# An attention and two-layer kernel: the first token pair in three blocks of 256 tokens, split out of PSUM, with four value buffers

## The chip, the cores and the metric

The kernel runs on one core of a Trainium2 chip. The core has TensorE (PE: matmuls and transposes into PSUM), VectorE (DVE), ScalarE (ACT), GpSimd (POOL) and SyncE (SP), which mostly issues DMAs; 16 DMA engines move data between device memory and the on-chip SBUF. Each engine works through its own list of instructions in order. The metric is the device time of one execution in microseconds (us); less is better.

## What is computed

Local attention with memory tokens, then two gated feed-forward layers, all in float32:

```python
# q, k, v: 4 x 8 heads x 768 x 64; mem_k, mem_v: 4 x 8 x 8 x 64
for c in range(768 // 32):                      # chunks of 32 queries
    k_full = [mem_k, k[32c-16 : 32c+40]]        # 8 + 56 keys, cut at the ends
    a = softmax(q_c @ k_full.T / 8); out_c = a @ v_full
x = out as 3072 tokens x 512
h = x @ w_in                                    # 512 -> 2048
x = (h * tanh(softplus(h))) @ w_out             # 2048 -> 512
xn = rms_norm(x) * rms_g
y = (silu(xn @ w_gate) * (xn @ w_val)) @ w_out2 # 512 -> 1536 -> 512
```

## The kernel before

**Precision.** A float32 operand is split into a high part rounded to fp32r and a low part that is the rest (`split`: ACT casts, DVE subtracts). A product of two operands is three matmuls: high x high, high x low, low x high (`product`, lines 639 to 641).

**Stages.** The 3072 tokens are four pairs of 768. For each pair attention runs in six tiles of 128 tokens and is followed by `x @ w_in`, whose result goes to device memory (`g_scratch`). The first pair uses plain products; pairs 2 to 4 use a scheme with seven products in place of eight on sums of blocks (`group1`), for which the operands are summed and split beforehand (`t_pieces`, the products 1, 6, 5, 4, 2, 7, 3 in this order). The later layers follow and don't concern the change. While PE works on one pair, the attention of the next is strung between its products (`slots`).

**Attention of tile t, step by step.** The names are used in all that follows.
- k, q, v loads (`load_k`, `load_q`, `load_v`; SP): 256-byte rows; a v tile is eight DMAs and, for some tiles, two of mem_v (8 KB each), which POOL then copies to three more places (`mem_v_copy`, line 385). k and q have two buffers each, v has two (`vw`).
- K (`k_pe`, line 395) and Q (line 438): four transposes each on PE into a bank; ACT and DVE copy them out (lines 404 to 412, 449). K of tile t + 1 completes the keys of tile t.
- S (line 458): scores, 64 small matmuls. DVE takes the maximum and subtracts (471, 472), ACT takes exp (477).
- P (line 490): four transposes; ACT copies (497).
- V (line 506): weights times values. DVE normalises (519 to 522).
- E (line 532): four transposes back. ACT copies them into the block `xb` (539).
K, Q, P and E share two PSUM banks (bk_86 and bk_87 in the order's rows, called `bk` in the trace), S and V share bkp.

**Products of the first pair.** A block is 384 tokens, three tiles. After its last E, `x_split` splits it in two halves of 256 features (four instructions of 768 columns). `unit(b, i)` multiplies block b by 256 columns of `w_in` (i = 0 to 7): 24 matmuls of 384 columns into two banks and two evictions by ACT (line 691). Three units of block 0 are strung into the attention of the first pair (`NHEAD`, `HEADS`), the other 13 run with the attention of pair 2 between them.

**Weights.** `w_in` is read as raw 64-bit halves of 512 KB (`load_raw`, issued by POOL, two buffers). The conversion `cv_all` takes each raw tile through ACT (202, 205), DVE (209, 210, 216) and a split (153, 154). Raw tiles are numbered here as they are loaded: 0 and 1 belong to i = 0, 2 and 3 to i = 1, and so on. In the first pair's attention six are converted (`CV_START` = 24 steps, four each).

**What sets the order.** A scheduler orders the instructions of each engine from the order in which the program emits them, by a timeline of its own; an instruction in `pin` keeps its place among pinned ones.

## Time and profile before

| | |
|---|---|
| time, median of 3 runs (least to most) | 1167.13 us (1166.1 to 1167.37) |
| the profiled execution: its time, its span | 1167.72 us, 1166.0 us |
| PE busy | 1140.7 us, 98% of the span |
| DVE, ACT, POOL busy | 823.8, 629.2, 183.4 us |
| mean granted clock of TensorE | 0.993 |

A busy PE is not always PE at its peak: the granted clock and the spacing of its instructions have to be read as well. The profile's rows give the start of an instruction or of a run of equal ones, how long they were on, and in square brackets how long the engine had been idle ahead of it and what released it. Starts are counted from the first instruction of the span.

### The profile page before, as it was taken

How to read it: one execution, taken by the hardware profiler on the slowest of the kernel's cores; microseconds unless marked ns; L12 is line 12 of the kernel's file. 1: busy time of each engine (PE TensorE's matmuls, PEld its weight loads, DVE VectorE, ACT ScalarE, POOL GpSimd, SP SyncE). 2: the span in 40 equal slices, each digit the busy share in tenths (PEclk: the TensorE clock that was granted, in tenths of full speed). 3: DMA queues.
4: the chain of work that ended last, by engine and by line, in shares of the span. 5: the costliest groups of instructions: out<-in, count | busy, mean ns of one | idle time of the engine just before them, and what ended most of it. 6: DMA issues, size and time to landing. Idle time of an engine off the chain costs nothing.

```text
span 1166.0 us, 22910 instructions
## 1 busy us (share of the span) xinstructions
PE 1140.7 (98%) x9052; PEld 1005.2 (86%) x9052; DVE 823.8 (71%) x1254; ACT 629.2 (54%) x1008; POOL 183.4 (16%) x165
## 2 busy tenths in 40 slices
...
GB/s 195 187 219 224 191 300 260 240 297 284 170 302 290 255 225 144 188 354 157 195 375 409 123 349 316 355 407 359 312 363 356 329 283 319 180 160 145 145 91 37
DMA packets 213276, 294.20 MB, mean 252 GB/s; under 512 B 104240, under 2 KB 160560, under 8 KB 204336
## 3 DMA queue, kind: packets, MB, share of 16 engines
...
## 4 chain that ended last, share of the span: by engine, by line
PE 75%; DMA 9%; DVE 8%; ACT 5%; issue 2%; POOL 0%; SPq 0%; ACTq 0%; DVEq 0%; POOLq 0%
PE bk L639 13%; PE bk L640 13%; PE bk L641 13%; DMA s<-g_scratch 4%; PE bk L912 4%; PE bk L914 4%; PE bk L913 4%; PE bk L755 3%; PE bk L756 3%; PE bk L754 3%; DVE T L154 2%; PE bkp L639 2%; PE bkp L640 2%; PE bkp L641 2%; PE bkp L506 2%
## 5 line engine op out<-in xcount | busy, mean ns | idle before, releaser
L639 PE MATMUL bk<-T,w 128*128 128x384 f32 (+1 forms) x860 | 315.6, 369 | 1.3 <-ACT c L657 1.0
L640 PE MATMUL bk<-T,w 128*128 128x384 f32 (+1 forms) x860 | 311.2, 362 | 0.0
L641 PE MATMUL bk<-T,w 128*128 128x384 f32 (+1 forms) x860 | 307.4, 361 | 0.0
L639 PEld LDWEIGHTS bk<-T,w 128*128 128x128 f32 x860 | 162.0, 189 | 21.0 <-ACT c L657 1.3
L640 PEld LDWEIGHTS bk<-T,w 128*128 128x128 f32 x860 | 161.9, 188 | 16.5 <-DVE T L154 0.3
L641 PEld LDWEIGHTS bk<-T,w 128*128 128x128 f32 x860 | 161.5, 188 | 15.8
L912 PE MATMUL bk<-w,T 128*128 128x256 f32 x396 | 112.1, 283 | 0.2 <-ACT T L153 0.2
L913 PE MATMUL bk<-w,T 128*128 128x256 f32 x396 | 112.0, 283 | 0.0
L914 PE MATMUL bk<-w,T 128*128 128x256 f32 x396 | 111.9, 283 | 0.0
L755 PE MATMUL bk<-T,w 128*128 128x512 f32 x276 | 107.5, 390 | 0.5 <-DVE T L154 0.5
L756 PE MATMUL bk<-T,w 128*128 128x512 f32 x276 | 107.1, 389 | 0.0
L754 PE MATMUL bk<-T,w 128*128 128x512 f32 x276 | 105.8, 389 | 0.0
L669 POOL TENSOR_TENSOR v<-c,v 128x512 f32<-128x512 f32 x36 | 54.1, 1503 | 291.7 <-DVE c L665 259.0
L665 DVE TENSOR_TENSOR c<-bk,c 128x512 f32<-128x512 f32 (+2 forms) x72 | 43.0, 598 | 54.5 <-PE bk L641 41.9
L912 PEld LDWEIGHTS bk<-w,T 128*128 128x128 f32 x396 | 76.0, 192 | 0.5 <-ACT T L153 0.4
L913 PEld LDWEIGHTS bk<-w,T 128*128 128x128 f32 x396 | 76.0, 192 | 0.0
L914 PEld LDWEIGHTS bk<-w,T 128*128 128x128 f32 x396 | 75.9, 192 | 0.0
L649 ACT COPY c<-bk 128x512 f32<-128x512 f32 (+2 forms) x72 | 36.9, 514 | 69.1 <-PE bk L641 25.3
L154 DVE TENSOR_TENSOR T<-s,T 128x1024 fp32r<-128x1024 f32 (+1 forms) x50 | 62.5, 1258 | 15.2 <-ACT T L153 15.1
L782 ACT ACTIVATE s<-s 128x1024 f32<-128x1024 f32 x44 | 46.4, 1059 | 31.3 <-DMA s<-g_scratch 31.2
L755 PEld LDWEIGHTS bk<-T,w 128*128 128x128 f32 x276 | 51.8, 188 | 11.6 <-DVE T L154 0.9
L756 PEld LDWEIGHTS bk<-T,w 128*128 128x128 f32 x276 | 51.8, 188 | 10.8
...
## 6 DMA issues: line engine op xcount, KB each, us to landing
...
```

Of the source, the lines that this page charges most:

```text
L154: keep((eng or nc.vector).tensor_tensor(lo, src, hi.bitcast(F32), op=ALU.subtract))
L639: nc.tensor.matmul(ps, whi, xh, start=first and kk == 0, stop=False, **more)
L640: nc.tensor.matmul(ps, whi, xl, start=False, stop=False, **more)
L641: nc.tensor.matmul(ps, wlo, xh, start=False, stop=kk == 1, **more)
L669: nc.gpsimd.tensor_tensor(c22, u3, z5, op=ALU.add)
L754: nc.tensor.matmul(ps, ahi, bhi, start=start, stop=False)
L755: nc.tensor.matmul(ps, ahi, blo, start=False, stop=False)
L756: nc.tensor.matmul(ps, alo, bhi, start=False, stop=stop)
L782: nc.scalar.activation(x, g, self.act)
L912: nc.tensor.matmul(ps, t[:, 0, f], w[:, 0], start=first and f == 0, stop=False, **more)
L913: nc.tensor.matmul(ps, t[:, 0, f], w[:, 1], start=False, stop=False, **more)
L914: nc.tensor.matmul(ps, t[:, 1, f], w[:, 0], start=False, stop=f == HG - 1, **more)
```

## The change

- The first pair becomes three blocks of 256 tokens (`NS`), two tiles each. A unit has 24 matmuls of 256 columns, into one bank, and one eviction of 512 columns (`unit_parts`); there are 24 units.
- The result of E is split straight out of PSUM by tile and half (`x_part`: one cast, one subtraction of 256 columns each); `xb` and `x_split` are not used in this pair.
- Two more value buffers, `v2`, lie in weight slot 1, which is free until its weights are converted; v2 and v3 go there. These two tiles load and copy mem_v as tiles 0 and 1 do.
- The start is emitted step by step from the list `START`. Each word is a step and its arguments: `lk lq va vb lr` are loads of k, q, the halves of v and raw weights; `K Q S P V E` are the steps above; `ka kb km kd qc pc` are copies out of PSUM; `mx sb ex z`, `nr nm` are parts of S's and V's follow-up; `mv` copies mem_v; `a` to `e` are the five steps of a conversion (ACT's two, DVE's two, DVE's add, ACT's cast, DVE's subtraction); `hi lo` are the split; `U.b.i` is a quarter of a unit, `g` its eviction, `st` its store. None of it is pinned.
- Eight raw tiles are converted in the start (`N_EARLY`), and six units run there: (0,0), (0,1), (1,1), (1,0), (1,2), (0,2). The other 18 follow with pair 2's attention, in an order of their own.

The bodies of `att_b1`, `att_d1` and `k_ev` are cut into parts with names and otherwise unchanged; this is left out of the diff.

```diff
-    jobs, raws, n_load, n_raw, start = [], [], [0], [10 ** 6], [True]
+    jobs, raws, n_load, n_raw, start = [], [], [0], [10 ** 6], [False]
...
+    def plain_steps(key, u, n):
+        raw = raws.pop(0)
+        if n == 0:
+            wslot[key] = w_slot(u)
+        w = as7(wslot[key])
+        hi, lo = (w[:, n:n + 3:2, l, :].rearrange("p e (k f) -> p k e f", k=2) for l in range(2))
...
+                if kind == "plain":
+                    done += 1
+                    if done <= N_EARLY:
+                        continue
+                    cv_prefetch(done - 1)
+                    steps = plain_steps(key, u, n)
+                    for c in "abcde":
+                        steps[c]()
+                        if c == "b":
+                            cv_prefetch(done)
+                        yield
+                    continue
                 cv_prefetch(done)
...
+    VS = NP * 4 * (D + 1)
+    v2 = w_slot(1)[:, 0:2 * VS].bitcast(F32)
+    v2 = [v2[:, VS * u:VS * u + VS].rearrange("p (a c d) -> p a c d", a=NP, c=4) for u in range(2)]
...
-    def load_v(t):
+    def load_v(t, halves=(0, 1)):
         b, i = divmod(t, SPB)
         s0 = 128 * i
-        vt = vw[t % 2]
-        vn[t] = vt
-        for h2 in range(2):
+        vt = vn[t] = v2[t - 2] if t in (2, 3) else vw[t % 2]
+        for h2 in halves:
             p0 = 64 * h2
-            if i < 2:
+            if i < 2 or t in (2, 3):
...
+    def att_c2(t):
+        att_c1(t)
+        mem_v_copy(t)
+
+    def att_d2(t):
+        att_d(t)
+        if t + 2 < TSUB:
+            load_v(t + 2)
...
-    def x_split(b, half):
-        t = t_new()
-        split(xb[b][:, 2 * half:2 * half + 2, :], t[:, 0], t[:, 1])
-        xtab[b, half] = t
-
-    xtab, n_unit = {}, [0]
+    NS = 256
+    NBS = 2 * N // NS
+    xs0 = []
+
+    def x_piece(b, half, l):
+        if not xs0:
+            xs0.extend(t_new().rearrange("p l a n -> p (l a n)") for _ in range(4))
+        t, at = (xs0[2 * b + half], 2 * NS * l) if b < 2 else (xs0[2 * half + l], 4 * NS)
+        return t[:, at:at + 2 * NS].rearrange("p (k n) -> p k n", k=2)
+
+    def x_part(t, half, l):
+        b, r = divmod(t, NS // 128)
+        src = st_e[t][:, 2 * half:2 * half + 2, :]
+        hi = x_piece(b, half, 0)[:, :, 128 * r:128 * r + 128]
+        if l == 0:
+            nc.scalar.copy(hi, src)
+        else:
+            lo = x_piece(b, half, 1)[:, :, 128 * r:128 * r + 128]
+            nc.vector.tensor_tensor(lo, src, hi.bitcast(F32), op=ALU.subtract)
+
+    n_unit, g_unit = [0], {}
...
+    def unit_parts(b, i):
+        w = wtab["i", i]
+        ps = bk[n_unit[0] % 4]
+        n_unit[0] += 1
+
+        def mul(e, half):
+            x = [x_piece(b, half, l) for l in range(2)]
+            ws = w[:, 2 * e + half].rearrange("p l (k f) -> p l k f", k=2)
+            out_ = ps[:, NS * e:NS * e + NS]
+            for kk in range(2):
+                end = half and kk
+                nc.tensor.matmul(out_, ws[:, 0, kk, :], x[0][:, kk, :],
+                                 start=not (half or kk), stop=False)
+                nc.tensor.matmul(out_, ws[:, 0, kk, :], x[1][:, kk, :], start=False, stop=False)
+                nc.tensor.matmul(out_, ws[:, 1, kk, :], x[0][:, kk, :], start=False, stop=bool(end))
+
+        def evict():
+            g = gp.tile([128, 2, N], F32, tag="g", name="g")[:, :, 0:NS]
+            nc.scalar.copy(g, ps.rearrange("p (e n) -> p e n", e=2))
+            g_unit[b, i] = g
+
+        dst = g_d[2 * i:2 * i + 2, :, NS * b:NS * b + NS].rearrange("f p n -> p f n")
+        return [lambda e=e, half=half: mul(e, half) for e in range(2) for half in range(2)], evict, dst
...
+    for n, x in enumerate(vw + v2):
+        if n < 2:
+            nc.gpsimd.memset(x, 0.0)
         nc.gpsimd.memset(x[:, :, :, D:D + 1], 1.0)
...
+    N_EARLY = 8
...
+    START = """
+        lk.0 lk.1 lq.0 lq.1 va.0 K.0 lr.0 ka.0 km.0 K.1 lr.1 kb.0 lk.2 kd.1 ka.1 km.1 Q.0 vb.0
+        kb.1 qc.0 Q.1 S.0 lk.3 va.1 qc.1 mx.0 a.0 sb.0 ex.0 b.0 lq.2 K.2 lq.3 z.0 vb.1 c.0 P.0
+        ka.2 mv.0 kd.2 S.1 d.0 kb.2 e.0 pc.0 K.3 lk.4 a.1 mx.1 va.2 kd.3 sb.1 Q.2 ka.3 b.1 V.0
+        ex.1 qc.2 vb.2 c.1 kb.3 mv.1 nr.0 P.1 d.1 nm.0 Q.3 pc.1 e.1 S.2 lr.2 lq.4 E.0 va.3 qc.3
+        mx.2 hi.0.0 K.4 sb.2 hi.0.1 mv.2 lo.0.0 ka.4 V.1 lo.0.1 ex.2 kd.4 vb.3 kb.4 nr.1 P.2
+        lr.3 a.2 nm.1 Q.4 S.3 pc.2 b.2 lk.5 E.1 qc.4 va.4 mx.3 hi.1.0 c.2 hi.1.1 mv.3 lo.1.0 d.2
+        lo.1.1 U.0.0 vb.4 a.3 sb.3 U.0.0 e.2 lr.4 ex.3 V.2 b.3 va.5 P.3 nr.2 K.5 lr.5 pc.3 c.3
+        U.0.0 ka.5 nm.2 U.0.0 d.3 lk.6 kd.5 V.3 kb.5 e.3 lq.5 g.0.0 vb.5 E.2 a.4 nr.3 U.0.1 nm.3
+        U.0.1 hi.2.0 b.4 hi.2.1 E.3 st.0.0 S.4 lk.7 hi.3.0 lo.2.0 lr.6 hi.3.1 lo.2.1 U.0.1
+        lo.3.0 lq.6 Q.5 lo.3.1 rg mx.4 U.0.1 lq.7 qc.5 c.4 K.6 g.0.1 U.1.1 sb.4 lk.8 d.4 st.0.1
+        U.1.0 kd.6 ex.4 e.4 S.5 a.5 P.4 mx.5 U.1.1 pc.4 b.5 U.1.0 U.1.1 sb.5 lr.7 U.1.0 c.5 ex.5
+        V.4 d.5 z.5 P.5 a.6 va.6 nr.4 U.1.1 e.5 U.1.0 nm.4 pc.5 U.1.2 b.6 g.1.1 V.5 g.1.0 vb.6
+        c.6 E.4 U.0.2 nr.5 hi.4.0 hi.4.1 nm.5 U.1.2 d.6 lo.4.0 U.0.2 st.1.1 a.7 lo.4.1 st.1.0
+        E.5 e.6 va.7 U.0.2 hi.5.0 b.7 U.1.2 hi.5.1 U.0.2 lo.5.0 lo.5.1 U.1.2 vb.7 g.0.2 c.7
+        g.1.2 d.7 e.7 st.0.2 st.1.2
+    """
...
+    with ExitStack():
+        for word in START.split():
+            name, *args = word.split(".")
+            start_ops[name](*map(int, args))
+    start[0] = True
+    cv_n[0] = 5 * N_EARLY
...
-    CV_I = 64
+    CV_I = 80
...
-    units = [(1, i) for i in range(NHEAD)]
-    units += [(b, i) for i in (3, 4, 7, 5, 6) for b in range(2)]
+    units = [(2, 0), (2, 2), (2, 3), (2, 1), (1, 3), (0, 3), (0, 4), (1, 4), (2, 4), (0, 7), (1, 7), (2, 7), (0, 5), (1, 5), (2, 5), (2, 6), (0, 6), (1, 6)]
     at = {u: 4 * n + 4 for n, u in enumerate(units)}
     more = {}
-    finish_at(more, 7, at[1, 7] + 1)
-    bt = slots((att_list(1), 4 * len(units)), (0, 73), tail_of(1), calls(more), CV_I)
+    finish_at(more, 7, max(at[b, 7] for b in range(NBS)) + 1)
+    bt = slots((att_list(1), 4 * len(units)), (0, 91), tail_of(1), calls(more), CV_I)
```

The order that the change gives, at three places. In the first, on POOL at the start of the program, `raw` is a raw weight tile and `COPY` a copy of mem_v. Before:

```order
L149 DMA raw<-in_moe_w_in_dram 128x2x512 x2
L931 MEMSET vw 128x16 x2
L385 COPY vw<-vw 8x4x195 x3
L149 DMA raw<-in_moe_w_in_dram 128x2x512
L385 COPY vw<-vw 8x4x195
L149 DMA raw<-in_moe_w_in_dram 128x2x512 x4
```

After (`w` is the weight slot that holds v2 and v3):

```order
L423 COPY vw<-vw 8x4x195
L149 DMA raw<-in_moe_w_in_dram 128x2x512
L423 COPY vw<-vw 8x4x195
L149 DMA raw<-in_moe_w_in_dram 128x2x512
L423 COPY vw<-vw 8x4x195 x2
L149 DMA raw<-in_moe_w_in_dram 128x2x512
L423 COPY w<-w 8x4x195 x3
L149 DMA raw<-in_moe_w_in_dram 128x2x512
L423 COPY w<-w 8x4x195
L149 DMA raw<-in_moe_w_in_dram 128x2x512 x4
```

Raws 2, 3, 4, 5 and 6 now each stand behind a copy of mem_v; before, raw 2 stands behind three, raw 3 behind one, and raws 4 to 6 behind none.

The second place is ACT late in the start, where the first unit's eviction comes (`g<-bk0_82`). Before, with `ca` and `lr` the two first steps of a conversion, `xb` the copy behind E, `p` an exp, `pT` the copy behind P:

```order
L202 ACTIVATE ca_735<-raw_549 128x512
L205 ACTIVATE lr_737<-raw_549 128x512
L691 COPY g_740<-bk0_82 128x384
L539 COPY xb_800<-bk4_86 128x4x128
L691 COPY g_740<-bk1_83 128x384
L477 ACTIVATE p_780<-p_780 128x512
L691 COPY g_875<-bk2_84 128x384
L153 CAST w_736<-ca_735 128x2x2x128
```

After, with raw_774 raw 6, raw_899 raw 7, and `CAST T` the high parts behind an E step:

```order
L200 ACTIVATE ca_948<-raw_774 128x512
L203 ACTIVATE lr_949<-raw_774 128x512
L452 COPY kw_108<-bk5_87 128x4x32
L793 COPY g_695<-bk0_82 128x2x256
L200 ACTIVATE ca_1059<-raw_899 128x512
L219 CAST w_947<-ca_948 128x2x2x128
L203 ACTIVATE lr_1060<-raw_899 128x512
L768 CAST T_426<-bk4_86 128x2x128
L768 CAST T_427<-bk4_86 128x2x128
L219 CAST w_947<-ca_1059 128x2x2x128
L793 COPY g_810<-bk1_83 128x2x256
```

Two raw tiles' conversions now stand among the first eviction, the casts that free bank 86 (bk4_86) and the second eviction; bank 86 is the one into which PE's next step, Q of tile 5, transposes.

The third place is PE where the first pair ends and `group1` begins (lines 639 to 641 before, 717 to 719 after, for its products). Before; the last E of pair 2 stands 24 products ahead of the first row of `kn`:

```order
L641 MATMUL bk3_85<-T_963,w_1914 128x384
L395 MATMUL bk5_87<-ident_89,kn_1758 128x128
L438 MATMUL bk4_86<-ident_89,qn_1571 128x128 x4
L395 MATMUL bk5_87<-ident_89,kn_1758 128x128 x3
L639 MATMUL bk0_82<-T_2129,w_1491 128x384
L640 MATMUL bk0_82<-T_2129,w_1491 128x384
L641 MATMUL bk0_82<-T_2129,w_1491 128x384
L639 MATMUL bk0_82<-T_2129,w_1491 128x384
L640 MATMUL bk0_82<-T_2129,w_1491 128x384
L641 MATMUL bk0_82<-T_2129,w_1491 128x384
L639 MATMUL bk1_83<-T_2145,w_1491 128x384
L640 MATMUL bk1_83<-T_2145,w_1491 128x384
```

After; the last E of pair 2 stands 20 products ahead of the first row with 384 columns:

```order
L789 MATMUL bk3_85<-T_427,w_1961 128x256
L717 MATMUL bk0_82<-T_2349,w_1442 128x384
L718 MATMUL bk0_82<-T_2349,w_1442 128x384
L719 MATMUL bk0_82<-T_2349,w_1442 128x384
L717 MATMUL bk0_82<-T_2349,w_1442 128x384
L718 MATMUL bk0_82<-T_2349,w_1442 128x384
L719 MATMUL bk0_82<-T_2349,w_1442 128x384
L433 MATMUL bk5_87<-ident_89,kn_1743 128x128 x4
L492 MATMUL bk4_86<-ident_89,qn_1747 128x128 x4
L717 MATMUL bk1_83<-T_2364,w_1442 128x384
L717 MATMUL bk2_84<-T_2373,w_1442 128x384
L718 MATMUL bk1_83<-T_2364,w_1442 128x384
```

K and Q move behind the first group product; T_2145 and T_2364 are the operands of the second one (product 6), whose low part is read by the matmul of line 640 before, 718 after.

## Rows read from the trace of the kernel before

**Rows 1.** The page, busy time, share of the span and instructions of each engine.
```profile
PE 1140.7 (98%) x9052; PEld 1005.2 (86%) x9052; DVE 823.8 (71%) x1254; ACT 629.2 (54%) x1008; POOL 183.4 (16%) x165
```

**Rows 2.** Stretches: length, busy us (x instructions) by engine, PE clock, DMA share, GB/s.
```profile
0.00:20.00 20.00, 11.73 (x224) 8.45 (x224) 4.18 (x10) 7.86 (x15) 5.89 (x15) 0.83 0.85 188
...
20.00:40.00 20.00, 13.41 (x376) 9.81 (x360) 13.65 (x27) 13.13 (x26) 4.34 (x5) 0.83 1.01 199
...
40.00:60.00 20.00, 18.60 (x354) 16.59 (x339) 13.22 (x27) 11.30 (x21) 1.45 (x2) 0.91 0.93 198
...
80.00:100.00 20.00, 20.00 (x317) 18.68 (x323) 11.54 (x24) 13.06 (x26) 2.89 (x4) 1.00 0.88 205
```

**Rows 3.** PE in order: start us, us, line, output<-inputs, count [idle before <-released by].
```profile
4.17 1.09 PE L395 MATMUL bk<-ident,kn 128*128 128x128 f32 x4 [4.17 <-DMA kn<-in_mem_k_dram]
...
31.27 0.63 PE L395 MATMUL bk<-ident,kn 128*128 128x128 f32 x4 [1.65 <-DMA kn<-in_k_dram]
...
42.85 0.87 PE L506 MATMUL bkp<-vw,pT 64*32 64x65 f32 x50 [0.79 <-DMA vw<-in_v_dram]
...
44.42 1.63 PE L639 MATMUL bk<-T,w 128*128 128x384 f32 x4
...
49.64 0.86 PE L458 MATMUL bkp<-kw,qT 64*32 64x64 f32 x64
...
50.43 0.66 PE L532 MATMUL bk<-ident,x 128*128 128x128 f32 x4
...
50.85 0.42 PE L640 MATMUL bk<-T,w 128*128 128x384 f32 x1
```

**Rows 4.** PE in order, at 75 us (384 columns) and 1050 us (256 columns).
```profile
75.05 0.33 PE L639 MATMUL bk<-T,w 128*128 128x384 f32 x1
...
76.09 0.33 PE L639 MATMUL bk<-T,w 128*128 128x384 f32 x1
...
1050.39 0.28 PE L912 MATMUL bk<-w,T 128*128 128x256 f32 x1
...
1051.11 0.28 PE L912 MATMUL bk<-w,T 128*128 128x256 f32 x1
```

**Rows 5.** DMA queues, first 65 us (packets, MB, share); raw weight tiles to landing.
```profile
q1 hardware_dynamic: 31474, 8.28, 69.1%
...
q0 software_dynamic: 1104, 4.06, 20.8%
...
DMA to landing us min/median/max: 4.4/5.4/7.3
```

**Rows 6.** POOL, ACT and DVE in order of time, same columns as rows 3.
```profile
11.88 0.82 POOL L385 COPY vw<-vw 8x780 f32<-8x780 f32 x1 [7.07 <-DMA vw<-in_mem_v_dram]
...
37.49 0.62 ACT L153 CAST w<-ca 128x512 fp32r<-128x512 f32 x1 [1.02 <-DVE ca L216]
...
39.43 0.67 ACT L205 ACTIVATE lr<-raw 128x512 int32<-128x512 uint32 x1
...
35.48 0.43 DVE L209 TENSOR_SCALAR ca<-ca 128x512 int32<-128x512 int32 x1 [1.31 <-ACT ca L202]
...
35.94 0.69 DVE L210 SCALAR_TENSOR_TENSOR ca<-raw,ca 128x512 int32<-128x512 int32 x1
...
154.44 0.40 ACT L153 CAST w<-sm 128x256 fp32r<-128x256 f32 x1
...
153.09 0.41 DVE L300 TENSOR_TENSOR sm<-ca,sm 128x256 f32<-128x256 f32 x1
```

**Rows 7.** PE and DVE in order of time where the token pair ends.
```profile
137.35 0.60 PE L532 MATMUL bk<-ident,x 128*128 128x128 f32 x4
...
141.78 0.34 PE L641 MATMUL bk<-T,w 128*128 128x384 f32 x1
...
144.22 0.44 PE L640 MATMUL bk<-T,w 128*128 128x384 f32 x1
...
143.22 0.94 DVE L154 TENSOR_TENSOR T<-g,T 128x768 fp32r<-128x768 f32 x1
```

223 lines of the change are left out of this document (127 added, 96 removed).

## The prediction, made before the changed kernel ran

> **What bounds the kernel now.** I read the page first, then the stretches, then PE's instructions in order of time. PE is busy for 98% of the span [rows 1]. By stretches it is not full only at the start: 11.7 and 13.4 us busy of 20 in the first two, at a granted clock of 0.83, and all of 20 from 80 us on [rows 2]. Behind the start PE has no gap worth the name, so a microsecond that PE loses or saves before about 140 us is lost or saved at the end. The reader should see in PE's rows what the start waits for: PE's first instruction comes at 4.17 us, k5 is awaited until 31.27, v3 until 42.85, and the first block product runs at 44.42 [rows 3]. The last block product starts at 141.78 [rows 7]. The change works between these times, so I forecast when the last block product starts and move the end by the same amount.
>
> **Prices on PE.** Six products of 384 columns take 1.04 us (75.05 to 76.09), 0.1733 each; six of 256 columns take 0.72 us (1050.39 to 1051.11), 0.120 each [rows 4]. A step of four transposes (K, Q, P or E) occupies PE for 0.42 us (50.43 to 50.85), a score or value step (S, V) for 0.79 (49.64 to 50.43) [rows 3].
>
> **Part 1, blocks of 256.** 8 x 2 x 24 = 384 products of 0.1733 become 8 x 3 x 24 = 576 of 0.120: 66.5 us become 69.1, **+2.6 us** on the engine that is full. The row decides here against a rule. The Trainium skill, TensorE: Matmul & The Clock Gate, section Back-to-back issue gap, gives N / 2.4 + 2.5 ns for an isolated matmul, 109 and 162.5 ns here; by that the term would be +0.4 us; the trace has 120 and 173.
>
> **Part 2, results split out of PSUM.** One ACT copy of 512 columns for each token tile and two copies and two subtractions of 768 columns for each block give way to two casts and two subtractions of 256 columns for each tile. That is less work on ACT and as much on DVE; neither is full in the start, so the saving is taken at nothing. A 256-column cast from PSUM has no row; the nearest is one from SBUF at 0.40, and the cast of 512 columns at 0.62 bounds it above [rows 6]; I take 0.40. What it costs is a tie: the bank of an E step stays taken until both casts and both subtractions are done.
>
> **Part 3, the first product earlier.** It needs two tiles in place of three. In the changed order PE runs K4, Q4, S3 and E1 ahead of it, so q4 must have landed. DMA is nearly full (share 0.85, 1.01, 0.93 [rows 2]), so I price by packets. Up to 65 us a packet of the SP queue took 0.691 x 65 x 16 / 31474 = 22.8 ns of an engine, 1.43 us for 1000 on 16 engines, and a raw weight tile 0.208 x 65 / 8 = 1.7 us [rows 5]. A k or q tile is 1024 packets, a v tile about 1790. On the kernel before: up to k5 it has 15872 packets and three raw tiles, 22.7 + 5.1 = 27.8, seen at 31.27, so 3.5 us of lead; v3 (20672 packets, five raws) comes to 41.6, seen at 42.85 [rows 3]. In the changed order q4 is packet 15712, with five raws ahead of it: 22.4 + 8.5 + 3.5 = **34.4 us**. Then Q4, S3, E1 (1.6), a cast (0.4) and hand-overs: first product at about **37**, 7 us earlier than now. From there to Q5 stand 44 products (5.3), V2, V3, P3, K5, E2 (2.8) and about 1.5 of low clock and hand-overs: PE reaches Q5 at **46.7**; k5 (40.1) and q5 (about 46) are there by then.
>
> **Part 4, the weights' conversion, which the scheduler pulls forward.** This decides. Engines run in order. On POOL the issue of raw 5 now stands behind copies of mem_v, the last of them for tile 3, whose 8 KB are queued just ahead of q4: landed at about 33. Such a copy waits for its DMA and takes 0.82 [rows 6], so raw 5 is issued at 33.9. From issue to landing a raw takes 4.4 to 7.3, 5.4 in the median [rows 5]: 39.3. Raw 7 needs raw 5's buffer: ACT's first step (0.67), then DVE's two (0.43 + 0.69) [rows 6]: issued at 41.2, landed at 46.6. ACT has raw 7's first step ahead of E2's casts: 47.3, a weight cast (0.62) 47.9, the second step (0.67) 48.5, two casts of 0.40: 49.3; DVE's two subtractions (0.41 each [rows 6]) end near 50. Only then is the bank free into which Q5 transposes. The next block's products wait still longer, for the eviction of bank 83, which stands behind raw 7's last cast: 51. I take **50.5** for Q5 in place of 46.7; PE has nothing else in its order, so 3.8 us stand idle. In the kernel before, a single copy stands on POOL among the issues of raws 2 to 6, and the first product waits for all three E steps anyway.
>
> **Part 5, the far end of the pair.** The sums over four blocks (early pieces of the next stage) begin when the last E step has been copied. Now: E at 137.35, the low half of the second group product's operand from 143.22, PE's matmul that reads it at 144.22 [rows 7], 6.9 us after E. PE covers that with 24 products of 0.1733 and other steps. In the changed order 20 products of 0.120 (2.4), one group product (1.04), K and Q (0.9), E itself (0.4) and two firsts (0.35) cover 5.1; with what is already waited now, about **+1.1 us**.
>
> **Part 6, value buffers.** Two more, in weight slot 1, let v2 and v3 load without waiting for V0 and V1: no PE wait there now but v3's landing [rows 3], so nothing by itself; their four mem_v loads and copies are priced in part 4.
>
> **The sum.** Before: at 44.42 there were left 66.5 of products, 4.1 of this pair's attention (S5, V4, V5 and four transposes), 20.0 of the next pair's (six tiles of 3.26 and a K): 90.6; 97.4 passed to 141.78, so 6.8 are lost to waits, low clock and changes of bank. After: from Q5 on there are left 532 x 0.120 = 63.8, 6.1 of this pair's attention, 20.0 of the next: 89.9. Of the 6.8 I keep 5.2, since the first products' low clock lies ahead of Q5 here, and add 1.1. 50.5 + 89.9 + 6.3 = 146.7, against 141.8: **+4.9 us**. The profiled execution took 1167.72, 0.59 above the median of the runs, 1167.13; the forecast goes to the median: 1172.0. The later stages keep their instructions and nearly their order, so nothing is added there.
>
> **Rivals.**
> - Raws land in time. For: an undisturbed raw took 4.4 us [rows 5], and two in chain save 2; if the queues also pause less (share 0.93 between 40 and 60 us [rows 2]) q4 comes 2 us earlier. Against: the changed start keeps both queues full, and then landings were above the median. The stall falls to about 0 to 1 us: Q5 at 46.5, end 142.7 to 143.2, +1 us, **1168**. Chance 0.16. Beside it stands a rule: the Trainium skill, DMA: Bandwidth & Descriptors, section Anatomy of one DMA, gives a GpSimd transfer 2.0 us and bytes / 436 GB/s, 3.2 us for 512 KB; by that raw 7 lands 4.4 us earlier and the stall is gone; the trace has 4.4 as its least.
> - Faster. The same, with the loads at the price of a queue that never pauses (about 7% of 31 us, 2.2) and the cover in part 5 found sufficient: first product at 34.5, Q5 at 44.3, end 44.3 + 89.9 + 4.2 = 138.4, -3.4 us, **1164**. It decides when q4 has landed by 32 and raw 7 by 43. Chance 0.10.
> - Worse. Raws at the long end, 7.3 each [rows 5]: 3.8 more, Q5 at 54.3, **1176**; a PE that has idled runs its next products at half clock, as in row 44.42, four in 1.63 us [rows 3]: up to 1.5 more. Chance 0.16.
>
> **How the numbers follow.** The forecast holds 0.58, with 1169.5 to 1174.5 as its own range. Eight in ten reach from 1166.5 (all of the first rival, a little of the second) to 1176.5. About 0.2% (2.3 us) is what a measurement can tell from no change: slower holds the forecast and the worse case, 0.74; same the first rival, 0.16; faster 0.10.
>
> **What would show it.** Right: the first product of 256 columns at 36 to 38 us; then a gap of 2 to 5 us on PE ahead of Q5 and the third unit's products, released by ACT or DVE; ACT idle before raw 7's first step until the DMA lands; a spacing of 0.120; the last block product at 145 to 148. Wrong: PE without a gap between 40 and 56 us (the raws came in time), or a first product after 40 us (the packet price is off), or a PE that waits in the middle of the 18 remaining units, which the rows of before give no ground for.

## The result: 14.6 us slower

| | before | after |
|---|---|---|
| time, median of 4 runs each (least to most) | 1167.25 us (1166.1 to 1169.55) | 1181.82 us (1180.11 to 1183.6) |
| ratio of the runs, 95% interval | | 1.0126 [1.0106, 1.0146] |
| span of the profiled execution | 1166.0 us | 1181.8 us |
| first block product starts | 44.42 us | 40.63 us |
| last block product starts | 141.78 us | 152.91 us |
| one and the same product of pair 2 | 240.92 us | 256.85 us |

The sign was forecast, the size was not: 4.9 us were expected, 1172, and the wider range (eight in ten) ended at 1176.5. The last row of the table is a product behind which both kernels have the same 4799 products of 256 or more columns. It comes 15.9 us later, and the span is 15.8 us longer, so all of the loss lies ahead of it: 11.1 us up to the last block product, 4.8 us behind it. The changed kernel's profiled execution is the longest of its four (1183.6), so these 15.9 us are 1.3 more than the 14.6 between the medians.

The busy times, which answer to [rows 1]:

```profile
PE 1143.6 (97%) x9244; PEld 1008.8 (85%) x9244; DVE 826.7 (70%) x1262; ACT 626.8 (53%) x1002; POOL 186.6 (16%) x171
```

The stretches that answer to [rows 2] (length, busy us and instructions of PE, PEld, DVE, ACT, POOL, then PE's granted clock, DMA share, GB/s):

```profile
0.00:20.00 20.00, 7.82 (x100) 5.47 (x100) 6.49 (x15) 9.44 (x17) 7.60 (x19) 1.00 0.91 191
20.00:40.00 20.00, 11.74 (x346) 8.73 (x344) 14.81 (x29) 11.94 (x23) 7.38 (x9) 0.91 0.98 193
40.00:60.00 20.00, 14.38 (x212) 13.29 (x211) 11.12 (x24) 9.29 (x19) 2.17 (x3) 0.84 1.12 203
80.00:100.00 20.00, 20.00 (x338) 19.06 (x338) 8.65 (x20) 12.40 (x25) 2.35 (x4) 1.00 0.89 223
```

PE is busy for 33.9 us of the first 60, where it was 43.7. From 80 us on it is full, as before. The rows that answer to [rows 3] and [rows 7], PE in order of time, say where it stands still; the pair at 152 us is for the pace:

```profile
37.02 1.09 PE L1099 MATMUL bk<-ident,qn 128*128 128x128 f32 x4 [3.77 <-DMA qn<-in_q_dram]
40.63 0.50 PE L786 MATMUL bk<-T,w 128*128 128x256 f32 x2 [0.46 <-ACT T L768]
55.26 1.11 PE L1099 MATMUL bk<-ident,qn 128*128 128x128 f32 x4 [5.15 <-DVE T L771]
...
152.19 0.28 PE L789 MATMUL bk<-T,w 128*128 128x256 f32 x1
...
152.91 0.28 PE L789 MATMUL bk<-T,w 128*128 128x256 f32 x1
...
155.28 0.44 PE L717 MATMUL bk<-T,w 128*128 128x384 f32 x1 [0.16 <-ACT T L153]
...
156.49 0.44 PE L717 MATMUL bk<-T,w 128*128 128x384 f32 x1 [0.77 <-ACT g L793]
...
256.85 0.42 PE L717 MATMUL bk<-T,w 128*128 128x384 f32 x1
```

L1099 is a Q step of the start: Q4 at 37.02, Q5 at 55.26. Q5 has stood 5.15 us behind DVE's subtraction of E2 (line 771), as the prediction said it would, only longer. What DVE waited for is seen on ACT, DVE and POOL (same columns; on POOL line 149 issues a raw tile and line 423 copies mem_v):

```profile
33.78 1.05 POOL L423 COPY w<-w 8x780 f32<-8x780 f32 x1 [4.09 <-DMA w<-in_mem_v_dram]
...
36.02 0.72 POOL L149 DMA_DIRECT2D raw<-in_moe_w_in_dram  x1
...
43.69 0.72 POOL L149 DMA_DIRECT2D raw<-in_moe_w_in_dram  x1 [3.73 <-DVE ca L210]
...
39.31 0.59 ACT L1106 COPY qT<-bk 128x512 f32<-128x512 f32 x1 [2.04 <-PE bkp L512]
40.21 0.65 ACT L768 CAST T<-bk 128x256 fp32r<-128x256 f32 x2 [0.31 <-PE bk L601]
...
41.31 0.65 ACT L200 ACTIVATE ca<-raw 128x512 f32<-128x512 f32 x1
...
51.34 0.66 ACT L200 ACTIVATE ca<-raw 128x512 f32<-128x512 f32 x1 [3.66 <-DMA raw<-in_moe_w_in_dram]
...
52.99 0.62 ACT L768 CAST T<-bk 128x256 fp32r<-128x256 f32 x2
...
54.49 0.71 DVE L771 TENSOR_TENSOR T<-bk,T 128x256 fp32r<-128x256 f32 x2
```

Raw 7 is issued at 43.69 and ACT starts on it at 51.34, 7.65 us later. E2 was done on PE at about 49, but its casts (line 768) stand behind raw 7's steps in ACT's list, at 52.99. The raw tiles of the first 65 us took, from issue to landing (least, median, most; [rows 5] had 4.4/5.4/7.3):

```profile
DMA to landing us min/median/max: 4.4/6.5/8.8
```

And the idling costs twice. Single microseconds around Q5, same columns as the stretches:

```profile
52.00:53.00 1.00, 0.00 (x0) 0.00 (x0) 0.93 (x2) 1.00 (x4) 0.00 (x0) 1.00 1.14 194
53.00:54.00 1.00, 0.00 (x0) 0.00 (x0) 1.00 (x4) 0.61 (x3) 0.26 (x1) 0.80 1.05 100
...
58.00:59.00 1.00, 1.00 (x7) 1.00 (x6) 0.00 (x0) 0.00 (x0) 0.00 (x0) 0.50 1.10 266
...
60.00:61.00 1.00, 1.00 (x12) 0.83 (x12) 0.00 (x0) 0.00 (x0) 0.00 (x0) 0.78 0.86 155
```

PE had been idle since 50.1; from 53.6 to 60.4 (0.80 and 0.78 are the means of the two slices in which it changes) the granted clock is 0.50, the lower of its two levels (1.2 GHz). PE is busy there from 55.26 on, so about 5.2 us run at half pace: some 2.6 us.

### The profile page after: what moved, and what is told of

The parts are those of the page before. It is cut to its first block, busy times and chain, and to the rows that moved or that the text cites. A ratio compares the mean times of both kernels' runs of the same rounds, so it can differ in the third digit from the quotient of the medians.

```text
span 1181.8 us, 23351 instructions
## 1 busy us (share of the span) xinstructions
PE 1143.6 (97%) x9244; PEld 1008.8 (85%) x9244; DVE 826.7 (70%) x1262; ACT 626.8 (53%) x1002; POOL 186.6 (16%) x171
## 3 DMA queue, kind: packets, MB, share of 16 engines
q8 instruction: 72, 1.18, 0.5%
## 4 chain that ended last, share of the span: by engine, by line
PE 78%; DMA 6%; DVE 6%; ACT 6%; issue 2%; SPq 1%; POOL 0%; ACTq 0%; DVEq 0%; POOLq 0%
PE bk L717 12%; PE bk L718 12%; PE bk L719 12%; PE bk L1024 4%; PE bk L1023 4%; PE bk L1022 4%; PE bk L865 3%; PE bk L866 3%; PE bk L864 3%; DMA s<-g_scratch 2%; PE bkp L717 2%; PE bkp L719 2%; PE bkp L718 2%; PE bk L786 2%; PE bk L788 2%
## 5 line engine op out<-in xcount | busy, mean ns | idle before, releaser
L717 PE MATMUL bk<-T,w 128*128 128x512 f32 (+1 forms) x732 | 271.0, 372 | 2.5 <-ACT g L793 0.8
L718 PE MATMUL bk<-T,w 128*128 128x512 f32 (+1 forms) x732 | 267.5, 365 | 0.1
L719 PE MATMUL bk<-T,w 128*128 128x512 f32 (+1 forms) x732 | 265.4, 365 | 0.0
L717 PEld LDWEIGHTS bk<-T,w 128*128 128x128 f32 x732 | 137.2, 188 | 22.8 <-ACT g L793 1.0
L718 PEld LDWEIGHTS bk<-T,w 128*128 128x128 f32 x732 | 137.6, 188 | 16.2 <-DVE T L154 0.3
L719 PEld LDWEIGHTS bk<-T,w 128*128 128x128 f32 x732 | 137.4, 188 | 15.7
L865 PEld LDWEIGHTS bk<-T,w 128*128 128x128 f32 x276 | 51.8, 188 | 12.1 <-DVE T L154 1.4
L864 PEld LDWEIGHTS bk<-T,w 128*128 128x128 f32 x276 | 51.7, 188 | 11.4 <-ACT T L153 0.6
```

What stands on the lines that cost most here:

```text
L717: nc.tensor.matmul(ps, whi, xh, start=first and kk == 0, stop=False, **more)
L718: nc.tensor.matmul(ps, whi, xl, start=False, stop=False, **more)
L719: nc.tensor.matmul(ps, wlo, xh, start=False, stop=kk == 1, **more)
L864: nc.tensor.matmul(ps, ahi, bhi, start=start, stop=False)
L865: nc.tensor.matmul(ps, ahi, blo, start=False, stop=False)
```

## The experiments

All kernels are edits of the changed kernel or of one another. Each was timed beside the kernel before on the same chip; the table has the ratio to it, and of each profiled execution its time, the last block product and the time from there to the product of the last row above (99.1 us before, 103.9 after). Executions of one kernel differ by 1 to 8 us, and behind the product of the last row alone the traces take 922.6 to 928.2 us. The last column is steady all the same: 103.8 to 104.3 in eight kernels. The last block product is not. lead leaves the start alone, and its trace has the same instructions in the same order on all five engines as the changed kernel's up to an E step at 76.90 us; yet in lead that step comes at 71.66, and the last block product 5.6 us earlier. Its profiled execution is the shortest of its six (1172.33 to 1180.37), that of the changed kernel the longest of its four. So a difference of that size in this column is not by itself the work of an edit; for the gain of an edit in the start the ratios count, and for the mechanism the rows. The intervals of tie, raw67, pin, mv, q4 and warm overlap that of the changed kernel, those of conv and lead and of all that combine them don't. Line numbers shift by up to four where an edit adds lines (Q is L1099, L1103 or L1105).

| kernel | median us (before beside it) | ratio, 95% interval | profiled execution us | last block product | from there to the product of pair 2 |
|---|---|---|---|---|---|
| changed kernel | 1181.82 (1167.25) | 1.0126 [1.0106, 1.0146] | 1183.6 | 152.9 | 103.9 |
| pin | 1179.72 (1167.76) | 1.0106 [1.0078, 1.0134] | 1182.15 | 152.4 | 104.0 |
| tie | 1178.72 (1167.76) | 1.0097 [1.0078, 1.0115] | 1179.01 | 147.3 | 104.3 |
| raw67 | 1177.32 (1167.76) | 1.009 [1.0066, 1.0113] | 1176.84 | 146.4 | 104.1 |
| conv | 1177.27 (1168.24) | 1.0065 [1.0043, 1.0088] | 1177.9 | 143.8 | 104.0 |
| mv | 1182.29 (1168.24) | 1.0106 [1.0072, 1.014] | 1181.96 | 152.8 | 103.9 |
| q4 (on raw67) | 1181.84 (1168.73) | 1.0112 [1.0089, 1.0135] | 1181.37 | 150.9 | 103.8 |
| warm (on raw67) | 1180.04 (1168.73) | 1.0101 [1.0076, 1.0126] | 1179.74 | 148.0 | 103.8 |
| lead | 1178.21 (1168.73) | 1.0074 [1.005, 1.0098] | 1172.33 | 147.3 | 100.3 |
| raw67lead | 1176.26 (1168.24) | 1.0065 [1.0043, 1.0087] | 1171.31 | 146.0 | 100.3 |
| all14 | 1172.55 (1168.24) | 1.0032 [1.0011, 1.0052] | 1174.55 | 147.6 | 100.2 |
| all14q5 | 1171.16 (1168.2) | 1.0029 [1.0016, 1.0042] | 1172.15 | 145.2 | 100.3 |
| convleadq5 | 1171.34 (1168.2) | 1.003 [1.0016, 1.0044] | 1168.66 | 143.2 | 100.3 |
| all18q5 | 1177.19 (1168.2) | 1.0087 [1.0069, 1.0105] | 1177.11 | 155.8 | 95.4 |

### Does raw 7 hold Q5? (tie, raw67, conv, pin)

**tie**: raws 6 and 7 keep their written place on ACT and DVE; their loads stay where they were.

```diff
+            start[0] = n >= 6
             halves[n][c]()
+            start[0] = False
```

> Only the conversion of raws 6 and 7 is kept in its written place on ACT and VectorE, behind E2's and E3's casts; every load stays. Theory A: the wait ahead of Q5 falls from 5.2 to under 1 us, Q5 at 50 to 51.5, total 1177 to 1178.5, though raw 7 lands as late as before. Theory B: the wait stays at 4 us or more with another releaser, total 1181 to 1183. If the weights of raws 6 and 7 are then late for the third unit after the pair's start (a wait on PE near 65 us), the gain is given back and the total stays at 1180 to 1182.

Measured: the wait ahead of Q5 is 1.18 us and its releaser is q5's own load.

```profile
52.95 0.63 PE L1099 MATMUL bk<-ident,qn 128*128 128x128 f32 x4 [1.18 <-DMA qn<-in_q_dram]
```

Raw 7 is issued at 42.88 and takes 8.5 us, so it lands at 51.4 as before; Q5 no longer waits for it. The expectation on Q5's time (50 to 51.5) was missed by 1.5, since q5 then lands last, and the median lies 0.2 above the range. The last block product comes 5.6 us earlier, no more than in lead without an edit of the start; by the ratios the gain is 3.4 us, with overlapping intervals.

**raw67**: raws 6 and 7 get buffers of their own (in `xb`, idle until pair 2) and are issued right behind raw 5.

```diff
+        raw = None
+        if n >= 6:
+            raw = atx.tile([128, KC, N], F32, tag="xb", name="xb").rearrange("p a n -> p (a n)")
+            raw = raw[:, 0:1024].bitcast(I32).rearrange("p (f t) -> p f t", t=2)
-        raws.append(load_raw(*flat[n]))
+        raws.append(load_raw(*flat[n], raw, *([pin] if n >= 6 else [])))
```

> Raws 6 and 7 get buffers of their own and are issued right behind raw 5, at about 36.5 us instead of 39.2 and 43.7; the order of the steps stays. Theory A in its form of the prediction (the chain of two raw landings): raw 7 lands at 43 to 46 instead of 51.3, Q5 at 49.5 to 51, total 1176.5 to 1178.5. Rival (three raws at once only share the DMA engines): raw 7 lands at 48 or later, q5 and k5 land later too, Q5 at 53 to 55, total 1180 to 1182.

Measured, on POOL the two issues, on PE the two waits next to each other in the list:

```profile
36.14 1.44 POOL L150 DMA_DIRECT2D xb<-in_moe_w_in_dram  x2
...
40.44 0.80 PE L786 MATMUL bk<-T,w 128*128 128x256 f32 x2 [0.46 <-DVE p L528]
...
70.82 0.65 PE L601 MATMUL bk<-ident,x 128*128 128x128 f32 x4 [0.78 <-DVE x L587]
```

Between 40.44 and 70.82 the trace shows no wait of PE; the last block product comes 6.5 us earlier (by the ratios 4.2 us are gained). ACT takes raw 7's first step at 46.22 without a wait. Q5 itself moved to 55.76, behind more products, so the expected 49.5 to 51 doesn't apply.

**conv**: all conversion steps of the start keep their written place.

```diff
-    jobs, raws, n_load, n_raw, start = [], [], [0], [10 ** 6], [False]
+    jobs, raws, n_load, n_raw, start = [], [], [0], [10 ** 6], [True]
```

> All conversion steps of the start (on ACT and VectorE) kept in their written place; loads, copies and PE left to the scheduler. It removes the pulling forward of all of them, where the kernel tie did so for raws 6 and 7 alone. Theory A: no cast of an E step waits behind a raw weight any more, Q5 at 49 to 51.5, total 1176 to 1178.5. Rival (the weights come later in turn, and the second and third unit wait for them): a wait on PE for w or T between 40 and 60 of 3 us or more, total 1179 to 1183.

```profile
49.80 0.66 PE L1099 MATMUL bk<-ident,qn 128*128 128x128 f32 x4
```

Q5 at 49.80 without a wait: theory A, by all its numbers. In this order q5 is there when PE comes to it. The last block product comes at 143.8, 9.1 us earlier, and by the ratios, whose intervals lie apart, 7.1 us are gained.

**pin**: every instruction of the start keeps its place among those of its engine, DMA issues too.

```diff
+    traced = nc.cur_bb.bb.instructions
+    first = len(traced)
...
+    for n, ins in enumerate(traced):
+        if n >= first and ins.engine in last:
+            tc.add_manual_dep(ins, last[ins.engine].name, ...)
+        last[ins.engine] = ins
```

> The start's steps stay on each engine in the order in which they are written; nothing else differs from the changed kernel. Theory A (the conversion steps that the scheduler pulled ahead are what costs the 5.2 us ahead of Q5): ACT does E2's and E3's casts before raw 7's first step, PE reaches Q5 at 49 to 51 us instead of 55.3, the last block product comes at 147 to 149 instead of 152.9, total 1176 to 1178. Theory B (PE would have waited there anyway, for DMA or for a backlog on ACT and VectorE): Q5 at 54 to 56, total 1180 to 1183. Theory C (the order of the whole start costs, not one wait): first product earlier than 40.6 as well, last block product before 145, total below 1174.

None of the three came whole: Q4 at 33.27 and the first product at 36.91 are as early as theory C and the prediction had them, and then Q5 waited 5.87 us for q5, which SP issues at 48.40 behind twelve pieces of v4 and v5.

```profile
48.40 0.39 SPq L397 DMA_DIRECT2D qn<-in_q_dram  x1
...
53.59 1.08 PE L1099 MATMUL bk<-ident,qn 128*128 128x128 f32 x4 [5.87 <-DMA qn<-in_q_dram]
```

So the wait ahead of Q5 is one on raw 7 through ACT (tie, raw67 and conv remove it in three ways), and it isn't enough to keep the written order: that order has another late load in the same place.

### Why is raw 7 late? (mv)

The prediction put it down to raw 5, issued behind POOL's copies of mem_v. **mv** moves raw 5's issue ahead of the four copies of tiles 2 and 3.

```diff
-  ... hi.0.1 mv.2 lo.0.0 ... hi.1.1 mv.3 lo.1.0 ... lr.4 ex.3 ... K.5 lr.5 pc.3 ...
+  ... hi.0.1 lo.0.0 ... hi.1.1 lo.1.0 ... lr.4 lr.5 mv.2 mv.3 ex.3 ... K.5 pc.3 ...
```

> The changed kernel with the issue of raw 5 moved ahead of the four copies of the memory values of tiles 2 and 3 on GpSimd; ACT, VectorE and PE keep their order but for a few rows. The prediction's chain (raw 7 is late because raw 5 is issued behind those copies): raw 5 issued at 28 to 29 instead of 36.0, raw 7 issued by 38 to 40 instead of 43.7 and landed by 46, Q5 at 50 to 52, total 1177 to 1179. Theory F (raw 7 is late because raw 5's first step stands on ACT behind the copy of Q4 and E1's casts, which come at 39.3 to 41.3 since q4 lands at 37.0): raw 5 lands much earlier and it does not matter; raw 7 issued at 42 to 44, landed 49 to 51, Q5 at 53.5 to 55.5, total 1180 to 1183.

```profile
28.90 0.72 POOL L149 DMA_DIRECT2D raw<-in_moe_w_in_dram  x1 [2.88 <-issue]
...
43.67 0.72 POOL L149 DMA_DIRECT2D raw<-in_moe_w_in_dram  x1 [4.03 <-ACT p L535]
...
54.87 0.66 PE L1099 MATMUL bk<-ident,qn 128*128 128x128 f32 x4 [2.43 <-DVE T L771]
```

Raw 5 is issued 7.1 us earlier and raw 7 at the same 43.67; the time doesn't move. (The wait ahead of Q5 is shorter only because PE comes to it later: its granted clock is 0.50 until 46.0 here and until 40.0 in the changed kernel.) Theory F holds: raw 5's first step (ACT at 41.31 in the rows of the changed kernel) stands without a wait of its own behind the copy of Q4 and E1's casts, and these wait for q4's landing at 37.0. But the prediction's chain was there too. In the changed kernel raw 5, issued at 36.02, took

```profile
DMA to landing us min/median/max: 5.1/5.1/5.1
```

and so landed at 41.1, 0.2 us before ACT came to it. The two chains end together, and to take one away gains nothing. So q4 alone is enough to delay raw 7, and raw 7 delays Q5; that raw 5's late issue would be enough as well is argued from the 41.1, no run has it without a late q4.

### Why is q4 late, and what does the clock cost? (q4, warm)

SP issued q4 at 33.39 only, 3.6 us ahead of its landing. **q4** (on raw67) was to issue k5 and q4 ahead of the second half of v2.

```diff
-  ... va.2 kd.3 sb.1 Q.2 ka.3 ... S.2 lr.2 lq.4 E.0 ...
+  ... kd.3 sb.1 Q.2 lq.4 va.2 ka.3 ... S.2 lr.2 E.0 ...      (lq.4 and va.2 in their written place)
```

> The kernel with own buffers for raws 6 and 7, and k5 and q4 issued ahead of the second half of v2 and of v3 instead of behind most of them. Theory E (q4 is late because its issue stands behind 56 KB and 8 KB pieces that go out one for each that lands, not because the packets ahead of it take long): q4 landed and Q4 at 32.5 to 33.5 instead of 36.7, first product at 36.5 to 37.5 instead of 40.4, the last block product 2 to 4 us earlier than 146.4, total 1173.5 to 1175.5. Rival (v2 and v3, and raws 5 to 7 behind their copies on GpSimd, come as much later): V2 or the second unit's products wait instead, total 1177 to 1179.

First q4's issue in raw67, then rows of q4:

```profile
30.39 0.39 SPq L397 DMA_DIRECT2D qn<-in_q_dram  x1
```
```profile
31.11 0.39 SPq L387 DMA_DIRECT2D kn<-in_k_dram  x1
31.60 0.53 SPq L397 DMA_DIRECT2D qn<-in_q_dram  x1
...
36.92 1.09 PE L1103 MATMUL bk<-ident,qn 128*128 128x128 f32 x4 [4.10 <-DMA qn<-in_q_dram]
...
45.62 0.65 PE L570 MATMUL bkp<-w,pT 64*32 64x65 f32 x20 [1.28 <-DMA vw<-in_v_dram]
```

A miss, and the edit didn't do what it was meant to do: q4 did not move in SP's list. In both kernels eleven loads stand between k4 and q4. In this one they are ten loads of `w` and k5; the ten must be v3's, since the edit keeps v2's behind q4. So q4 goes out no earlier than in raw67, Q4 starts at 36.92 (36.74 there), and v2 and the copies behind it come later: V2 waits three times, 3.7 us in all, up to 45.62, and the last block product is 4.5 us later. Theory E was not tested, and what q4's landing hangs on is not settled. Over the kernels of the table Q4 starts between 32.9 and 37.3, and with the same lists on all engines 2.1 us apart (37.0 in the changed kernel, 34.9 in lead).

**warm** (on raw67) fills PE's wait ahead of Q4 with 48 transposes of the identity into banks that nobody reads; they are added work.

```diff
+        for n in range(48 if t == 4 else 0):
+            pin(nc.tensor.transpose(bk[n % 4][:, 0:128], ident, ident))
```

> The kernel with own buffers for raws 6 and 7, and 48 transposes of the identity, into banks that nobody reads, on PE ahead of Q4, where PE otherwise stands still from 31.4 to 36.7 us and then has a granted clock of 0.50 until 45 us. They are added work whose results are not used. If the idling costs the clock: the clock stays 1.00 from 34 to 45, of the 3.9 us that it costs 3 to 4 come back, total 1173.5 to 1175. If the half clock comes regardless of what PE does: no change, 1176.5 to 1178.5. If the added work outlasts the wait (48 x 0.105 = 5.0 us, against a wait of 5.3): up to 1 us worse than this.

Stretches of 2 us, first of raw67, then of warm:

```profile
33.00:35.00 2.00, 0.00 (x0) 0.00 (x0) 1.70 (x3) 1.13 (x3) 0.96 (x2) 0.93 0.65 98
37.00:39.00 2.00, 2.00 (x69) 1.50 (x68) 0.40 (x2) 0.00 (x0) 1.54 (x3) 0.50 0.87 279
```
```profile
33.00:35.00 2.00, 2.00 (x21) 2.00 (x20) 1.28 (x2) 0.55 (x1) 1.96 (x3) 1.00 0.44 98
37.00:39.00 2.00, 1.34 (x68) 1.01 (x67) 0.00 (x0) 0.19 (x1) 0.53 (x1) 1.00 1.03 247
```
```profile
38.81 0.66 ACT L200 ACTIVATE ca<-raw 128x512 f32<-128x512 f32 x1 [3.74 <-DMA raw<-in_moe_w_in_dram]
...
40.84 0.50 PE L786 MATMUL bk<-T,w 128*128 128x256 f32 x2 [2.49 <-ACT T L768]
```

The idling does cost the clock: with PE busy it stays at 1.00 to 42.9 us, where raw67 has 0.50 from 34.7. But the time isn't gained: the median, 1180.04, lies above all that was expected. The scheduler had put another raw's first step ahead of E1's casts (ACT at 38.81), the first product came no earlier (40.84), and behind that wait of 2.49 us the clock fell to 0.50 after all, from 42.9 to 46.3.

### The loss behind the pair (lead, all18q5)

Eight kernels with quite different starts all took 103.8 to 104.3 us from the last block product to the same product of pair 2 (99.1 before). DVE tells why: stretches of 13 us ahead of the last block product, of before, of the changed kernel and of lead.

```profile
129.00:142.00 13.00, 13.00 (x200) 12.54 (x182) 9.39 (x18) 6.27 (x12) 4.13 (x4) 1.00 0.75 181
```
```profile
140.00:153.00 13.00, 13.00 (x224) 12.51 (x223) 5.24 (x11) 3.74 (x7) 2.79 (x4) 1.00 0.57 144
...
170.00:190.00 20.00, 19.52 (x296) 18.00 (x295) 19.58 (x38) 12.96 (x26) 6.00 (x7) 1.00 0.92 281
190.00:210.00 20.00, 18.41 (x286) 16.25 (x285) 18.31 (x36) 11.72 (x25) 5.30 (x6) 1.00 0.90 217
```
```profile
134.00:147.00 13.00, 13.00 (x168) 12.74 (x167) 8.62 (x14) 5.08 (x11) 3.81 (x4) 1.00 0.63 162
```

In the changed kernel DVE (third pair of numbers) is busy 5.24 us of the 13, where it had 9.39: the sums wait for an E that comes 2.7 us ahead of the last block product (4.4 before, [rows 7]). Behind it DVE is nearly full, 19.58 of 20 us, so it doesn't catch up, and PE loses 1.6 of 20 us as late as 190 to 210. **lead** starts the sums 14 slots (four to a unit) ahead of the end in place of 7, and so the attention that they need.

```diff
-            span = n_slots - 7
+            span = n_slots - lead
-            if n >= n_slots - 7 and tail:
+            if n >= n_slots - lead and tail:
-    bt = slots((att_list(1), 4 * len(units)), (0, 91), tail_of(1), calls(more), CV_I)
+    bt = slots((att_list(1), 4 * len(units)), (0, 91), tail_of(1), calls(more), CV_I, 14)
```

> The changed kernel with the attention of the second pair and the sums over its four blocks set 7 slots of PE's work earlier (14 slots ahead of the end of the first pair's units, not 7). Four kernels so far lose 9.8 to 10.3 us against PE's pace in the 100 us behind the last block product, the kernel before 5.75. Theory D (the sums come late to the far end of the pair, and VectorE carries the delay for 50 us): the loss behind the last block product falls to 5.5 to 6.5, total 1177 to 1178.5, with Q5 still at about 55. Rival (VectorE is full there whatever the sums do, 18 to 19.6 us busy of 20): the loss stays at 9 to 10, total 1181 to 1183; if the earlier attention makes PE wait inside the units, 1183 to 1185.

3.6 of the 4.8 us come back (100.3), whatever the start: lead, raw67lead, all14, all14q5 and convleadq5 all have 100.2 or 100.3. Of both figures 0.4 us are work that only changes its place, one K step, which the kernel before and lead do ahead of the last block product and the changed kernel behind it; 4.4 lost and 3.2 regained are left. Theory D holds, though 6.9 us of loss are left against PE's pace, a little more than the 5.5 to 6.5 expected. Q5 was expected at 55 and came at 52.31, with the same wait in kind, though the start is not edited:

```profile
48.25 0.70 ACT L200 ACTIVATE ca<-raw 128x512 f32<-128x512 f32 x1 [0.21 <-DMA raw<-in_moe_w_in_dram]
...
52.31 0.66 PE L1099 MATMUL bk<-ident,qn 128*128 128x128 f32 x4 [1.80 <-DVE T L771]
```

Raw 7 landed 3.1 us earlier than in the changed kernel's execution. So of the 6.1 us that lead gains by the ratios the edit explains the part behind the pair; the rest is not shown to be its work. **all18q5** goes to 18 slots:

> As the first of this batch, with the sums 11 slots earlier than in the changed kernel instead of 7. If the sums are still late (6.9 us are lost behind the last block product, 5.75 in the kernel before): the loss falls to 5.5 to 6.2, total 1 us less than the first of this batch, 1167 to 1169. If what is left there is VectorE's load: the same as the first, or up to 2 us slower because the attention of the second pair crowds the units.

Behind the last block product there is then nothing to win back (95.4), but the attention crowds the units: the last block product comes 10.7 us later than in all14q5, and the whole is 6 us slower, where 2 at most were expected. Part of that is work moved from behind to ahead; what counts is the product of pair 2, 251.2 against 245.4. Of these 5.8 us 2.9 are there at Q5 already (52.91 against 49.97), with the same lists in the start; for the rest the crowding is argued, not shown.

### Together (raw67lead, all14, all14q5, convleadq5)

**raw67lead** has both edits.

> Own buffers for raws 6 and 7, and the sums over the four blocks 7 slots earlier: the two edits that gained alone, together. If they cost at different places (ahead of Q5 and behind the pair), the gains add: 4.5 and 3.6 us, total 1173 to 1175, loss behind the last block product 6.5 to 7.5. If the one only lets the other's wait come later, total 1177 to 1178.

The last block product is as in raw67 and the part behind it as in lead, so the two places look independent; the median, 1176.26, is still 1.3 us above the range expected. **all14** adds the written order of the conversions.

> Own buffers for raws 6 and 7, all conversion steps in their written place, and the sums 7 slots earlier. If the pulled conversions still hold ACT anywhere with the buffers of raws 6 and 7 (they stood ahead of E1's casts for raw 4 and raw 5), it takes off another 1 to 3 us: total 1171 to 1173. If what is left is the landing of q, the blocks of 256 and PE's clock, it is as the kernel with the two edits, 1173 to 1175. The kernel before takes 1167 to 1169 on the same chip; only a gain of 12 us or more on the changed kernel would beat it.

1172.55: another 3.7 us. PE's longest wait behind 40 us is now the one that pin had:

```profile
50.88 1.09 PE L1103 MATMUL bk<-ident,qn 128*128 128x128 f32 x4 [3.11 <-DMA qn<-in_q_dram]
```

**all14q5** issues q5 ahead of v4's eight pieces and leaves PE's list alone; **convleadq5** is the same without the two extra raw buffers.

```diff
-  ... lk.5 E.1 qc.4 va.4 ... kb.5 e.3 lq.5 g.0.0 ...
+  ... lk.5 lq.5 E.1 qc.4 va.4 ... kb.5 e.3 g.0.0 ...      (lq.5 and va.4 in their written place)
```

> The kernel with own buffers for raws 6 and 7, conversions in their written place and the sums 7 slots earlier, and the issue of q5 ahead of the eight pieces of v4. PE's order is the same row for row. If q5's landing is the next late transfer: the wait of 3.1 us ahead of Q5 goes, and about 1 us of half clock behind it, total 1168 to 1170, at the kernel before or within 2 us of it. If k5, v3 or a cast then waits instead: 1171.5 to 1173.

> The same without the own buffers for raws 6 and 7. If the order of the conversions is what matters and the landing of raw 7 not: within 1 us of the kernel with the buffers, 1168 to 1171. If raw 7's landing still holds something (the third unit's weights, or ACT in its written place): 2 us or more slower, 1172 to 1174.

```profile
48.92 0.66 PE L1099 MATMUL bk<-ident,qn 128*128 128x128 f32 x4
...
243.44 0.42 PE L717 MATMUL bk<-T,w 128*128 128x384 f32 x1
```

That is convleadq5: Q5 at 48.92 without a wait, and the product of pair 2 at 243.44 instead of 256.85. The gain of moving q5 is within the measurement (1.0029 against 1.0032, 1171.16 between the two ranges expected), though the wait is gone: in the profiled execution of all14q5 q4's wait is 4.77 us instead of 2.33. The extra buffers make no difference once the order is kept. Against lead (1.0074) the written order with q5's move (1.003) gains 5.1 us, and the intervals lie apart. With three edits 11.4 of the 14.6 us are back. No version beats the kernel before: the best two are 3 us behind it, which is about the price of the 256-column products (2.6) and what is left behind the pair (1.1); that is a sum of two figures, no run takes the blocks alone.

### Two runs that say nothing on the value buffers (two, twof)

Both put v2 and v3 back into two buffers without their mem_v loads and copies; in the second the loads are written behind V0 and V1.

```diff
-        vt = vn[t] = v2[t - 2] if t in (2, 3) else vw[t % 2]
+        vt = vn[t] = vw[t % 2]
```

> Two value buffers in place of four: the loads of v2 and v3 wait for V0 and V1 again, and the four loads and four copies of the memory values of tiles 2 and 3 are gone. Theory A with the prediction's chain (raw 5's issue stands behind those copies): raw 5 issued by 31 instead of 36.0, raw 7 landed by 46 instead of 51.3, Q5 at 50 to 52, total 1177 to 1179. Rival (v2 and v3 come later and hold P and E steps): first product at 42 or later, total 1181 to 1184.

> The changed kernel with two value buffers: the loads of v2 and v3 are written behind V0 and V1, and the four loads and four copies of the memory values of tiles 2 and 3 are gone. Prediction's part 4 (the issue of raw 5 stands behind those copies on GpSimd): raw 5 issued by 31 to 32 instead of 36.0, raw 7 landed at 44 to 47 instead of 51.3, Q5 at 50 to 52, total 1177 to 1179. Rival (v2 and v3 come later than PE needs them): V2 or V3 waits for DMA by 1 us or more, total 1180 to 1183.

In `START` the loads of v2 and v3 stand ahead of V0 and V1, and those of v4 and v5 ahead of V2 and V3. With two buffers a tile's weights are therefore applied to the values of a later tile, and V waits for that tile's load: 1185.85 and 1184.07 us, with waits of V0 for v in the first. What the buffers are worth was not measured.

## Why the prediction was wrong in size

**Part 1, the blocks: right.** Six products from 152.19 to 152.91 are 0.120 each, as [rows 4] had it; the 2.6 us stand as spacing times count.

**Part 2, the split: right.** Two casts of a tile take 0.65 together on ACT, two subtractions 0.71 to 0.76 on DVE, less than the 0.80 and 0.82 assumed. The tie of the bank to them is what Q5 waited on.

**Part 3, the first product: 3.6 us off.** It was forecast at 37 and came at 40.63: 2.6 us since q4 landed at 37.0 and not at 34.4, 1.0 since Q4, S3 and E1 then ran at half clock. The failing step is the price by packets, "22.4 + 8.5 + 3.5": it assumes that the queue always has work ahead. The changed SP list doesn't give it that: in the changed kernel one wait of SP for q3's landing lasts 2.3 us, q4 goes out at 33.39, and the DMA share is 0.82 between 30 and 35 us. In lead's execution, with the same list, q4 goes out at 31.19 and Q4 starts at 34.94, so the size of this error is in part that of one execution. From the first product to where PE stops ahead of Q5 (50.1) it took 9.5 us; 9.7 were forecast.

**Part 4, the conversion: the right wait for half of the reason, and 4.8 us too short.** Forecast: raw 7 issued at 41.2, landed at 46.6, Q5 at 50.5. Measured: 43.69, 51.34, 55.26. The last leg, from the landing through ACT and DVE to Q5, is exact (3.9 both times). The issue is 2.5 us late. The step named, raw 5's issue behind POOL's copies, was there (36.02, 33.9 forecast), but mv takes it away and nothing moves: raw 5's steps stand behind q4's work on ACT, which the prediction left out of this chain, so part 3's error comes in here and is enough. The landing took 7.65 instead of the median 5.4 (2.3 us); the bound of 7.3 was in the "worse" rival, the median was the wrong row for a tile that lands where both queues are full (share 1.12). The same section of the Trainium skill that stood with the first rival (DMA: Bandwidth & Descriptors, Anatomy of one DMA) gives 3.2 us for it as an estimate from its figures; in the changed kernel's first 65 us nothing landed under 4.4.

**Part 5, the end of the pair: 1.1 us forecast, 4.8 measured (4.4 without the K step that changes its place).** The wait at the change of stage is there (0.16 and 0.77 us in the rows at 155 and 156). What failed is the sentence "the later stages keep their instructions and nearly their order, so nothing is added there". DVE's work there fills its time, so sums that begin late stay late for 50 us; lead shows it.

**The sum.** From Q5 to the last block product 97.6 us passed, 96.2 were forecast; the 1.1 of part 5, which the forecast had put ahead of the last block product, came behind it, and the half clock behind Q5 (2.6) came instead, which leaves 1.4 or 1.5. So 15.9 - 4.9 = 11.0 missing us are 4.8 (Q5) + 1.4 (clock) + 4.8 (behind the pair). Between the medians 9.8 are missing.

**What is the execution's.** These rows are of the changed kernel's longest execution. In lead's shortest, with the same lists in the start, Q4 starts at 34.94, the first product at 38.65, raw 7 lands at 48.2, Q5 starts at 52.31 and the last block product at 147.31, where 34.4, 37, 46.6, 50.5 and 146.7 were forecast. So the forecast of the start came near to what one execution did, and that of the part behind the pair was wrong in all of them. lead's other five executions took 3.3 to 8.0 us more than this one, the changed kernel's other three 0.3 to 3.5 less than the one shown. How much of the miss in the start is the list's and how much the execution's, and what makes the loads land late in one and not in another, stays open.

**Rivals and range.** "Raws land in time" and "faster" stood for the opposite of what came. "Worse" had the mechanism, with one raw at 7.3 and the half clock, and ended at 1176; it had no part for a late q4 nor for the far end. The range took the raw's bounds and gave q4, the change of stage and the spread between executions (3.5 us in the changed kernel, 8.0 in lead) none above the forecast: that is why it missed.

**What would show it.** The gap ahead of Q5 released by DVE, ACT idle before raw 7 and the spacing of 0.120 were seen as forecast; the first product after 40 us was named as the sign that the packet price is off, and it came, though in lead's execution of the same lists it was 38.65.
